# New durations in the price table of a kernel's own list scheduler: a gated scan and two layers on one core

## The chip, the core and the metric

The kernel runs on one core of one Trainium2 chip. The time is the device time of one execution in microseconds; of several runs the median counts.

## The reference

A linear-attention scan over 4 sequences of 768 tokens with 8 heads (32 columns each, a state of 16 rows), then root-mean-square normalisation and a gated layer of 1536 hidden units, then a second layer of 2048 hidden units with squared relu. Shortened to what is computed:

```python
def _attn_ref(x, a, B, C) -> np.ndarray:
    ...
    log_a = np.log(np.clip(a, 1e-06, 1.0))
    state = np.zeros((batch, H, N, D), dtype=np.float32)
    for c in range(nc):
        ...
        cum = np.cumsum(la, axis=-1)
        L = np.exp(cum[:, :, :, None] - cum[:, :, None, :]) * causal
        M = np.einsum('bhin,bhjn->bhij', Cc, Bc) * L
        y[:, :, sl] = (np.einsum('bhij,bhjd->bhid', M, xc)
                       + np.einsum('bhin,bhnd->bhid', Cc, state) * decay_to_i)
        state = decay_full * state + np.sum(Bx, axis=2)
    return y

def _moe_ref(x, w_gate, w_val, w_out, rms_g):
    xn = x / np.sqrt(np.mean(x * x, axis=-1, keepdims=True) + 1e-06) * rms_g
    g = xn @ w_gate
    return (g * (1.0 / (1.0 + np.exp(-g))) * (xn @ w_val)) @ w_out

def _moe2_ref(x, w_in, w_out, s, b):
    r = np.maximum(x @ w_in, 0.0)
    return (s * (r * r) + b) @ w_out

def reference(...):
    attn_out = _attn_ref(x, a, B, C)
    x = attn_out.transpose(0, 2, 1, 3).reshape(3072, 256)
    return _moe2_ref(_moe_ref(x, ...), ...)
```

`x` is (4, 8, 768, 32), `a` (4, 8, 768), `B` and `C` (4, 8, 768, 16); the 3072 tokens then have 256 columns. All inputs are float32; the weights of the layers come as float64.

## The kernel before

**The scan.** The 3072 tokens are cut into 32 chunks of 96 tokens, eight chunks to a sequence, and a chunk's 8 heads are done together. A chunk goes through five steps. `scan` (L381) loads the factors and multiplies them up on VectorE in one instruction over 896 columns (`a<-a,delta`). `gram` (L392) forms the products of B and C on TensorE (`g`) and multiplies them onto the factors on VectorE. `outs` (L413) forms the chunk's output `y` and its next state in eight small products, and ScalarE copies it out (`yt`). `back` (L432) turns it over on TensorE (two transposes, `y<-ident,yt`), copies the state for the next chunk (`xh`), and normalises: ScalarE squares and sums (`xn,ss`), POOL makes the factor in two steps on one column (`ss`, `rs`), and VectorE scales (`xn<-y,rs,gb`; for the first four chunks ScalarE does it). `turn` (L455) turns the normalised chunk back on TensorE (`y<-ident,xn`), and ScalarE and VectorE split it into a high and a low part (`xth`, `xtl`) for the layers. From chunk 7 on `split_bc` (L361) first splits B and C into parts (`hs`, `fb`, `fc`). The bank for `y` exists once: the next chunk's `y` waits until `xth` and `xtl` have been read out of it.

**The layers.** Tokens go in 8 blocks of 384 columns, four chunks each. A product of float32 precision is three products of rounded parts (`three`, L543). `hidden1` and `out1` do layer one, with 12 tiles of 128 hidden units, `hidden2` and `out2` layer two with 16. The first block (`hidden1_plain`, L596) uses plain float32 products in two halves, while the float64 weights are loaded and decoded (`decode`, L487: `e`, `sg`, `raw`, then `w1f` on VectorE and ScalarE). After that the two layers alternate (L713); the chunks of a coming block are scanned while layer two of an earlier one runs, in stretches of about 33 us.

**What sets the order.** The kernel's code is run once against a recorder, `Plan` (L49). Each instruction is written down with a duration from `price` (L140), and with the instructions that it needs. `issue` (L256) then works out starts with a list scheduler: `forward` (L178) starts, engine by engine, the ready instruction with the earliest "latest start", `backward` (L233) works the latest starts out again from the end, three times over, and the best of the three passes is kept. Only the order within each engine reaches the chip; the hardware's semaphores do the waiting. On TensorE products of ones are put into gaps that the schedule shows before the first use of the bank `o0` (L281 to L286), as many as fit the gap at 0.056 us each; they keep the engine going and write into a bank that is not yet used:

```python
while busy + self.FILL + 0.05 < start[i]:
    self.nc.tensor.matmul(out=idle, lhsT=ones, rhs=ones, start=True, stop=True)
    busy += self.FILL * (2 if busy < self.COLD else 1)
```

The price of an instruction thus has two effects: where it and others stand in their engines' queues, and how many products of ones there are. Nearly every instruction is issued from one line, L288 before and L289 after the change.

Of the kernel before, what the change touches and what calls it, by code (L numbers as in the profile page):

```python
# [8 lines left out]
F32 = mybir.dt.float32  # L9
# [10 lines left out]
P = 128  # L20
CH = 96            # tokens of a chunk of the scan
NST = 16           # rows of the scan's state
R = CH + NST       # a chunk's rows: its tokens, then the state
NH = 8
HD = 32
NCHUNK = 32
CPB = 8            # chunks of a batch row
NBLK = 8           # blocks of tokens of the two layers
BCH = NCHUNK // NBLK
N = BCH * CH  # L30
PLAIN = range(7)   # first chunks whose products of B and C are plain float32 ones
LAG = 2
F1 = 12            # tiles of 128 hidden units, first and second layer
F2 = 16
DM = 256
NCLIP = 2          # first chunks whose factors are clipped after they are spread over the rows
SIZE = {F32: 4, F32R: 4, I32: 4, U32: 4, BF16: 2, I16: 2, U16: 2, I64: 8}
EMIN = 916         # a weight's power of two is kept times 2**-20: 16 bits, biased by 127

# [9 lines left out]
class Plan:  # L49
    """Takes instructions down in program order, works out which need which, and issues every  # L50
    engine's in the order in which a list scheduler starts them: of the instructions that are
    ready the one that is to be started first, by the paced products that wait for it."""

    WRITES = ("out", "accum_out")
    FIRST_OUT = ("transpose", "memset", "tensor_copy", "tensor_scalar_mul")
    SEM = 0.13          # us from an instruction's end to a waiting one's start
    DMA_LEAD, DMA_TAIL, DMA_ISSUE, DMA_RATE = 1.1, 0.85, 0.45, 360e3
    BEGIN = 0.6
    COLD = 3.5          # until then the tensor engine runs at half its clock
    FILL = 0.056        # a product in a gap of the tensor engine  # L60
    HOLD = 2.0          # how much longer than the gap left a more urgent instruction may be held up
    STICK = 0.03        # gap in which the next product of a group of small ones is waited for
    PASSES = 3
# [26 lines left out]

    # which bytes of a tile an operand covers: its partitions, and a mask of 4-byte words
    def cover(self, ap):
# [47 lines left out]
    def price(self, eng, fn, args, kw):  # L140
        out = kw.get("out", args[0] if args else None)
        n = out.free_size()
        aps = [a for a in list(args) + list(kw.values()) if hasattr(a, "tensor")]
        psum = any("PSUM" in str(a.space) for a in aps)
        if fn == "dma_start":
            return max(0.06, out.nbytes() / self.DMA_RATE)
        if eng == "tensor":
            if fn == "transpose":
                return max(n / 1.2, 80) / 1e3 + 0.005
            w, four = kw["lhsT"], SIZE[kw["lhsT"].dtype] == 4 and kw["lhsT"].dtype == F32  # L150
            cols = w.free_size()
            if out.start_partition():
                return 0.053
            return max((4 if four else 1) * n / 2.4, (1.64 if four else 0.8) * cols) / 1e3 + 0.003
        if eng == "scalar":
            extra = sum(k in kw and hasattr(kw[k], "tensor") for k in ("scale", "bias", "accum_out"))
            return (n / 1.2 + (51 if psum else 93) + 93 * extra) / 1e3
        if eng == "vector":
            sizes = [SIZE[a.dtype] for a in aps if a.free_size() > 1]
            fast = not psum and fn in ("tensor_scalar", "tensor_copy", "memset")  # L160
            fast = fast or (fn == "tensor_tensor" and not psum and max(sizes) == 2)
            more = 62 if fn == "scalar_tensor_tensor" and hasattr(kw["scalar"], "tensor") else 0
            return (n / (1.92 if fast else 0.96) + 67 + more) / 1e3
        if fn == "tensor_tensor":
            return 0.46
        if fn == "tensor_scalar":
            return 0.16
        return n / 1.15e3 + 0.04
# [7 lines left out]

    # starts and ends, of the ready instructions the one that is to start first going ahead
    def forward(self, succs, late):  # L178
# [52 lines left out]

    # the latest starts with every engine's work in line: a schedule of the same kind from the end
    def backward(self, succs, start, end):  # L233
# [22 lines left out]
    def issue(self, idle):  # L256
        ops = self.ops
        succs = [[] for _ in ops]
        for op in ops:
            for p, lag in op["preds"].items():  # L260
                succs[p].append((op["i"], lag))
        # the latest start that the paced products ask for
        late = [0.0] * len(ops)
# [7 lines left out]
        for _ in range(self.PASSES):  # L271
            start, stop = self.forward(succs, late)
            found.append((max(stop), start, stop))
            late = self.backward(succs, start, max(stop))
        _, start, stop = min(found, key=lambda f: f[0])
        # products of ones in the tensor engine's gaps keep its clock up, until idle is needed
        ones = self.nc.const_aps.tensor(1.0, (P, P), BF16)
        until = min(start[op["i"]] for op in ops if getattr(op["kw"].get("out"), "name", None) == idle.name)
        busy = self.BEGIN
        for op in sorted(ops, key=lambda o: (start[o["i"]], o["i"])):  # L280
# [6 lines left out]
            engine = getattr(self.nc, op["eng"] if op["eng"] != "dma" else "sync")  # L287
# [3 lines left out]
def place(c, h):  # L291
    # where a head's matrix lies: the plain products of even and of odd heads go to two banks
    return h % 2 * 4 + h // 2 if c in PLAIN else h


@with_exitstack
def scan_glu_relu2(ctx: ExitStack, tc: tile.TileContext, bc, xr, aa, cst, w1, w2, gn, sv, bv, out):
# [20 lines left out]
    cst_sb = const.tile([P, 4], F32, name="cst_sb")  # L318
    fc = const.tile([P, 4, 2, R], F32R, name="fc")
    gb = const.tile([CH, DM], F32, name="gb")  # L320
    sb = const.tile([P, 6], F32, name="sb")
# [13 lines left out]

# [1 line left out]
    bc_t, a_t, x_t, f_t, y_t, yt_t, xn_t = {}, {}, {}, {}, {}, {}, {}  # L337
# [21 lines left out]

    # rows of B: hi hi lo lo, of C: hi lo hi lo; a pair of heads has one product  # L360
    def split_bc(c):  # L361
# [112 lines left out]
    def stream():  # L474
        # a chunk's steps lie between those of the chunks before and after it
        s = []
        for c in range(NCHUNK):
            fs = [scan, gram, outs, back, turn]
            at = [2, 4, 7, 9, 11]
            if c not in PLAIN:  # L480
                fs, at = [split_bc] + fs, [0] + at
            s += [(6 * c + t, c, f) for t, f in zip(at, fs)]
        s.sort(key=lambda e: e[0])
        return [(c, f) for _, c, f in s]

# [1 line left out]
    def decode(raw, out, n):  # L487
        # words of a float64: low 32 bits; sign, exponent (11 bits), top 20 bits of the fraction
        low = raw.bitcast(U32).rearrange("p (n w) -> p n w", w=2)[:, :, 0]
# [5 lines left out]
        sg = dec_p.tile([P, 6 * P], BF16, tag="sg", name="sg")[:, :n]  # L495
        # the power of two as the bits of a bfloat16, zero below its range
        nc.vector.tensor_scalar(out=e, in0=top_u, scalar1=0x7FF0, scalar2=None, op0=ALU.bitwise_and)
        nc.scalar.activation(out=e, in_=e, func=AF.Relu, scale=8.0, bias=emin)
        nc.scalar.activation(out=sg, in_=top_i, func=AF.Sign)
        # the mantissa, 2**20 and up  # L500
        nc.vector.tensor_scalar(
            out=high, in0=high, scalar1=0xFFFFF, scalar2=0x100000,
# [3 lines left out]
            out=man, in0=low, scalar=2.0 ** -32, in1=high, op0=ALU.mult, op1=ALU.add  # L506
# [21 lines left out]

    # the second layer's weights stay in the place of their words until they are split
    def decode2(m):  # L530
# [8 lines left out]

# [1 line left out]
    pending = deque()  # L541
# [52 lines left out]

    # the first block, with plain float32 products, in two halves
    def hidden1_plain(j, m, half):  # L596
# [32 lines left out]

    # a further column of ones in the first block sums w2_out's columns  # L630
    def out2(j, m, hi, lo):
# [22 lines left out]
    def drain(n):  # L654
# [10 lines left out]

    # constants
    nc.gpsimd.memset(delta, 0.0)
    nc.gpsimd.affine_select(
        out=delta[0:CH], in_=delta[0:CH], compare_op=ALU.not_equal, fill=1.0, base=0,
# [5 lines left out]
        out=ident, in_=ident, compare_op=ALU.not_equal, fill=1.0, base=0,  # L675
# [17 lines left out]

    # the first block of both layers and the weights, the second block's first layer
    o_t[0, 1] = new_o()
# [6 lines left out]
    for i in range(F1 + behind):  # L702
# [6 lines left out]
        if i >= behind:  # L709
            hidden1_plain(0, i - behind, 1)  # L710
            drain(LAG)
    # the other phases: layer 1 of a block two phases ahead of its layer 2
    phases = [(1, 1), (1, 2), (2, 0), (2, 1)]  # L713
# [6 lines left out]
    start = {(layer, j): i for i, (layer, j, m) in reversed(list(enumerate(plan)))}  # L720
# [88 lines left out]
```

## Time and profile before

| | before |
|---|---|
| time, median of 3 runs | 691.07 us |
| the three runs | 687.67, 691.08, 691.07 us |
| the profiled execution: span from first to last instruction | 687.0 us |
| the profiled execution: its own time from end to end | not given beside its span |
| instructions | 11407 |
| TensorE (PE) busy | 659.5 us, 96% |
| VectorE (DVE) busy | 470.4 us, 68% |
| ScalarE (ACT) busy | 371.1 us, 54% |
| GpSimd (POOL) busy | 65.9 us, 10% |
| products of ones on TensorE | 144 |

Busy shares are means over stages with different limits: the stretches by time say which engine is full where. A wait is put down to the instruction whose end came last. A granted clock of 1.00 is TensorE's upper level, 2.4 GHz, and 0.50 its lower, 1.2 GHz. Products are pipelined, so the time of one in the list is longer than the distance from one to the next.

### The profile page before, as it was taken

What the parts mean: (1) busy time and instruction counts of PE and PEld (TensorE: products, weight loads), DVE (VectorE), ACT (ScalarE), POOL (GpSimd) and SP (SyncE); (2) the same over time, 40 slices, a digit from 0 to 9 for tenths busy, and PEclk for the clock granted to TensorE, in tenths of its full rate; (3) what the DMA queues carried; (4) which work ended last, traced back from release to release, by engine and by line L of the source; (5) the groups of instructions that cost most, each with busy time, mean ns of one, the idle gap of its engine ahead of it and who ended that gap; (6) DMA issues with size and microseconds to landing.
All of it is one profiled execution on the core that took longest, in us unless ns stands there. A gap on an engine that the chain in (4) does not pass through costs nothing.

```text
span 687.0 us, 11407 instructions
## 1 busy us (share of the span) xinstructions
PE 659.5 (96%) x4332; PEld 630.4 (92%) x4332; DVE 470.4 (68%) x832; ACT 371.1 (54%) x780; POOL 65.9 (10%) x112
## 2 busy tenths in 40 slices
PE   8899899999999989999999999999899999999997
PEld 7688699899999879998899989999799998999997
DVE  6789999999997895348933597346963485334443
ACT  3686645667776654356533574346643564335544
POOL 3301210300010130002100030001200011000000
PEclk9899999999999999999999999999999999999999
DMA  8789732300001331004210042002320010000000
GB/s 256 236 294 338 273 113 74 125 1 0 2 1 51 112 113 50 1 1 142 66 42 0 30 141 79 1 1 68 112 68 1 1 59 7 18 1 1 1 23 24
DMA packets 19222, 50.30 MB, mean 73 GB/s; under 512 B 3104, under 2 KB 8576, under 8 KB 19168
## 3 DMA queue, kind: packets, MB, share of 16 engines
q1 hardware_dynamic: 19168, 49.58, 22.4%
q8 instruction: 34, 0.56, 0.3%
q14 instruction: 20, 0.16, 0.1%
HBM read 46.31 MB, written 3.26 MB: 72 GB/s over the span
## 4 chain that ended last, share of the span: by engine, by line
PE 41%; issue 41%; POOL 8%; DVE 6%; ACT 2%; DMA 1%; POOLq 0%; ACTq 0%; DVEq 0%
PE h L288 22%; PE o L288 17%; POOL ss L288 4%; POOL rs L288 4%; DVE a L288 2%; PE y L288 1%; DVE raw L288 1%; DVE e L288 1%; DVE w1f L288 1%; ACT xn L288 1%; DMA a<-in_aa 1%; PE g L288 1%; DMA a<-a_scr 1%; DVE h L288 0%; ACT e L288 0%
## 5 line engine op out<-in xcount | busy, mean ns | idle before, releaser
L288 ACT ACTIVATE s<-h 128x384 f32<-128x384 f32 x212 | 104.1, 491 | 141.3 <-PE h L288 107.9
L288 PE MATMUL h<-x,w2hl 128*128 128x384 f32 x768 | 164.9, 341 | 0.0
L288 DVE TENSOR_TENSOR lo<-s,hi 128x384 fp32r<-128x384 f32 x212 | 117.7, 555 | 39.0 <-ACT hi L288 31.2
L288 PEld LDWEIGHTS h<-x,w2hl 128*128 128x128 f32 x768 | 135.2, 188 | 2.2 <-issue 2.1
L288 PE MATMUL o<-hi,w2hl 128*128 128x384 f32 (+1 forms) x512 | 134.3, 341 | 0.0
L288 PE MATMUL h<-xtl,w1h 128*128 128x384 f32 x336 | 113.3, 337 | 0.9 <-DVE xtl L288 0.9
L288 PE MATMUL h<-xth,w1h 128*128 128x384 f32 x336 | 113.1, 337 | 0.0
L288 PE MATMUL h<-xth,w1l 128*128 128x384 f32 x336 | 113.1, 337 | 0.0
L288 DVE TENSOR_TENSOR s<-h,s 128x384 f32<-128x384 f32 x84 | 46.6, 555 | 70.6 <-PE h L288 66.9
L288 DVE CAST hi<-s 128x384 fp32r<-128x384 f32 x128 | 45.4, 356 | 71.4 <-ACT s L288 69.8
L288 PEld LDWEIGHTS o<-hi,w2hl 128*128 128x128 f32 x512 | 91.9, 188 | 1.6 <-issue 1.4
L288 PE MATMUL o<-lo,w2hl 128*128 128x384 f32 (+1 forms) x256 | 87.2, 343 | 0.0
L288 ACT CAST hi<-s 128x384 fp32r<-128x384 f32 x84 | 43.2, 514 | 78.9 <-DVE s L288 78.6
L288 POOL TENSOR_SCALAR ss<-ss 96x1 f32<-96x1 f32 x32 | 30.2, 943 | 425.8 <-ACT xn L288 424.5
L288 ACT ACTIVATE s<-s 128x384 f32<-128x384 f32 x128 | 67.2, 525 | 3.1
L288 DVE TENSOR_TENSOR_SCAN a<-a,delta 112x896 f32<-112x896 f32 x32 | 64.6, 2019 | 1.3 <-DMA a<-a_scr 1.0
L288 PEld LDWEIGHTS h<-xtl,w1h 128*128 128x128 f32 x336 | 63.1, 188 | 1.9 <-DVE xtl L288 1.5
L288 PEld LDWEIGHTS h<-xth,w1l 128*128 128x128 f32 x336 | 63.1, 188 | 0.2 <-issue 0.2
L288 PEld LDWEIGHTS h<-xth,w1h 128*128 128x128 f32 x336 | 63.1, 188 | 0.0
L288 PE MATMUL o<-lo,w1h 128*128 128x384 f32 x168 | 57.4, 342 | 0.0
L288 PE MATMUL o<-hi,w1h 128*128 128x384 f32 x168 | 56.5, 337 | 0.0
L288 PE MATMUL o<-hi,w1l 128*128 128x384 f32 x168 | 56.4, 336 | 0.0
(68 smaller groups left out, 842.3 us busy)
## 6 DMA issues: line engine op xcount, KB each, us to landing
a<-a_scr SPq DMA_DIRECT2D x30, 392.0 KB, 3.6
bc<-in_bc SPq DMA_DIRECT2D x25, 448.0 KB, 3.8
raw<-in_w SPq DMA_DIRECT2D x12, 768.0 KB, 5.2
raw<-in_w SPq DMA_DIRECT2D x16, 512.0 KB, 6.1
xh<-in_xr SPq DMA_DIRECT2D x32, 96.0 KB, 3.4
out_t<-ob SPq DMA_DIRECT2D x16, 192.0 KB, 1.9
a<-in_aa SPq DMA_DIRECT2D x2, 392.0 KB, 4.9
bc<-in_bc SPq DMA_DIRECT2D x14, 56.0 KB, 5.0
```

Source lines behind the costliest of these rows:

```text
L288: getattr(engine, op["fn"])(*op["args"], **op["kw"])
```

## The change

The prices in `price` are set anew, and nothing else. A product of rounded parts over n columns costs n/2.285 + 6 ns where it was n/2.4 + 3 (384 columns: 174 ns, before 163). ScalarE's base is 60 and 100 ns instead of 51 and 93; an instruction that also sums costs 230 ns more instead of 93, and one that writes fewer than 32 partitions 120 more. VectorE's scan counts twice its columns: 896 columns cost 1.93 us, before 1.00. On POOL the two-input step (`rs`) costs 0.6 us instead of 0.46, and the step with constants (`ss`, one column) falls to the general rule, 0.04 us instead of 0.16. The rest of the diff takes comments away.

```diff
@@ -147,24 +147,25 @@
         if eng == "tensor":
             if fn == "transpose":
                 return max(n / 1.2, 80) / 1e3 + 0.005
-            w, four = kw["lhsT"], SIZE[kw["lhsT"].dtype] == 4 and kw["lhsT"].dtype == F32
+            w, four = kw["lhsT"], kw["lhsT"].dtype == F32
             cols = w.free_size()
             if out.start_partition():
                 return 0.053
-            return max((4 if four else 1) * n / 2.4, (1.64 if four else 0.8) * cols) / 1e3 + 0.003
+            return max(4 * n / 2.4 + 5 if four else n / 2.285 + 6, (1.64 if four else 0.8) * cols) / 1e3
         if eng == "scalar":
-            extra = sum(k in kw and hasattr(kw[k], "tensor") for k in ("scale", "bias", "accum_out"))
-            return (n / 1.2 + (51 if psum else 93) + 93 * extra) / 1e3
+            extra = 93 * sum(k in kw and hasattr(kw[k], "tensor") for k in ("scale", "bias"))
+            extra += 230 if "accum_out" in kw else 120 if out.ap[0][1] < 32 else 0
+            return (n / 1.2 + (60 if psum else 100) + extra) / 1e3
         if eng == "vector":
             sizes = [SIZE[a.dtype] for a in aps if a.free_size() > 1]
             fast = not psum and fn in ("tensor_scalar", "tensor_copy", "memset")
             fast = fast or (fn == "tensor_tensor" and not psum and max(sizes) == 2)
             more = 62 if fn == "scalar_tensor_tensor" and hasattr(kw["scalar"], "tensor") else 0
+            if fn == "tensor_tensor_scan":
+                n *= 2
             return (n / (1.92 if fast else 0.96) + 67 + more) / 1e3
         if fn == "tensor_tensor":
-            return 0.46
-        if fn == "tensor_scalar":
-            return 0.16
+            return 0.6
         return n / 1.15e3 + 0.04
 
     def lasts(self, op, now):
```

The set of instructions is the same but for the products of ones, of which there are now 196 instead of 144. Before, they stand in runs of 33, 43, 7, 15, 3, 15, 20, 7 and 1, all but the last one ahead of the first product of layer one; now in runs of 33, 45, 28, 13, 54 and 13 ahead of those, and 3 and 7 behind the first. POOL's order does not change. On TensorE, VectorE and ScalarE about half the instructions or more change their place, most by a few places; on the queue of SyncE 79 of 156 do.

VectorE in chunk 5 (`a_228` is the factors of chunk 6, `xn_237` the normalised chunk 5, `raw1_279`, `e_281` and `w1f_280` the decoding of the last weight tile of layer one), before:

```order
L288 TENSOR_SCALAR raw1_279<-raw1_279 128x768
L288 TENSOR_TENSOR h32_266<-h_265,h32_266 128x192
L288 SCALAR_TENSOR_TENSOR raw1_279<-raw1_279 128x768
L288 TENSOR_TENSOR e_281<-e_281,sg_282 128x768
L288 SCALAR_TENSOR_TENSOR a_228<-a_228,delta_106 112x896
L288 TENSOR_TENSOR w1f_280<-raw1_279,e_281 128x768
L288 SCALAR_TENSOR_TENSOR xn_237<-y_226,rs_239,gb_104 96x256
```

and now:

```order
L289 TENSOR_SCALAR raw1_279<-raw1_279 128x768
L289 SCALAR_TENSOR_TENSOR a_228<-a_228,delta_106 112x896
L289 SCALAR_TENSOR_TENSOR raw1_279<-raw1_279 128x768
L289 TENSOR_TENSOR e_281<-e_281,sg_282 128x768
L289 TENSOR_TENSOR h32_266<-h_265,h32_266 128x192
L289 TENSOR_TENSOR w1f_280<-raw1_279,e_281 128x768
L289 SCALAR_TENSOR_TENSOR xn_237<-y_226,rs_239,gb_104 96x256
```

The scan of the next chunk stands three instructions earlier.

VectorE at the third chunk under layer two of block 3 (`xn_868` is that chunk, number 18; `a_863` the factors of the next), before:

```order
L288 TENSOR_TENSOR lo_895<-s_893,hi_894 128x384
L288 SCALAR_TENSOR_TENSOR fc_103<-bc_848,cst_sb_102,hs_851 64x4x112 x2
L288 SCALAR_TENSOR_TENSOR a_863<-a_863,delta_106 112x896
L288 CAST hi_901<-s_900 128x384
L288 SCALAR_TENSOR_TENSOR xn_868<-y_857,rs_870,gb_104 96x256
```

and now:

```order
L289 CAST hi_901<-s_900 128x384
L289 TENSOR_TENSOR lo_895<-s_893,hi_894 128x384
L289 SCALAR_TENSOR_TENSOR a_863<-a_863,delta_106 112x896
L289 SCALAR_TENSOR_TENSOR fc_103<-bc_848,cst_sb_102,hs_851 64x4x112 x2
L289 SCALAR_TENSOR_TENSOR xn_868<-y_857,rs_870,gb_104 96x256
```

The scan stands ahead of the two `fc` steps, no longer behind them, and `hi_901` ahead of both. At the last chunk of the stretch, number 19, the scan of the chunk after it now stands directly ahead of `xn_908`, where a `lo` step and an `fc` step lay between.

TensorE at that last chunk (`h_924` and `h_925` are the first products of layer one's next block), before:

```order
L288 MATMUL o0_846<-hi_913,w2hl_643 128x384 x2
L288 MATMUL y_897<-ident_107,xn_908 128x96
L288 MATMUL o0_846<-lo_914,w2hl_643 128x384
L288 MATMUL y_897<-ident_107,xn_908 128x96
L288 MATMUL o1_847<-hi_913,w2hl_643 128x384 x2
L288 MATMUL o1_847<-lo_914,w2hl_643 128x384
L288 MATMUL o0_846<-hi_918,w2hl_649 128x384 x2
L288 MATMUL h_924<-xth_789,w1h0_111 128x384
L288 MATMUL h_924<-xth_789,w1l_306 128x384
```

and now:

```order
L289 MATMUL o0_846<-lo_914,w2hl_643 128x384
L289 MATMUL o1_847<-hi_913,w2hl_643 128x384 x2
L289 MATMUL o1_847<-lo_914,w2hl_643 128x384
L289 MATMUL y_897<-ident_107,xn_908 128x96 x2
L289 MATMUL o0_846<-hi_918,w2hl_649 128x384 x2
L289 MATMUL h_924<-xth_789,w1h0_111 128x384
L289 MATMUL h_924<-xth_789,w1l_306 128x384
L289 MATMUL h_925<-xth_789,w1h0_111 128x384
```

The two transposes of the chunk stand together, three products further back, and two products instead of five lie between them and the first product that reads `xth`. At the third chunk 16 products instead of 13 lie between the transposes of `yt` and those of `xn`, at the last one 16 instead of 17.

## Rows read from the trace of the kernel before

**Rows 1.** The page, busy time, share of the span, instructions.
```profile
PE 659.5 (96%) x4332; PEld 630.4 (92%) x4332; DVE 470.4 (68%) x832; ACT 371.1 (54%) x780; POOL 65.9 (10%) x112
```

**Rows 2.** Chain that ended last: start, us, what; six products.
```profile
182.21 1.05 PE o L288 x6
```

**Rows 3.** Stretches: length, busy us (instructions) of PE, PEld, DVE, ACT, POOL; clock; DMA.
```profile
0.00:40.00 40.00, 33.03 (x347) 28.53 (x348) 29.26 (x38) 22.53 (x46) 13.07 (x21) 0.87 0.79 239
40.00:140.00 100.00, 93.56 (x670) 85.00 (x669) 96.60 (x158) 61.76 (x132) 15.45 (x17) 1.00 0.57 198
140.00:215.00 75.00, 74.96 (x428) 74.67 (x427) 71.78 (x150) 54.05 (x104) 3.40 (x32) 1.00 0.02 7
215.00:580.00 365.00, 354.63 (x2304) 339.22 (x2303) 229.68 (x401) 184.89 (x406) 33.99 (x42) 1.00 0.17 52
```

**Rows 4.** Waits of PE: who waited for whom, us in total, times, longest.
```profile
PE y L288 <- DVE xn L288: 12.4, 16, 1.4
PE y L288 <- ACT xn L288: 3.9, 3, 2.1
```

**Rows 5.** Timeline, chunk 5: the scan, POOL, the transpose that waits.
```profile
73.35 2.01 DVE L288 TENSOR_TENSOR_SCAN a<-a,delta 112x896 f32<-112x896 f32 x1
...
73.73 2.54 POOL L288 TENSOR_SCALAR ss<-ss 96x1 f32<-96x1 f32 x1 [5.75 <-ACT xn L288]
...
77.46 0.38 PE L288 MATMUL y<-ident,xn 96*128 96x96 f32 x2 [1.21 <-DVE xn L288]
```

**Rows 6.** All ss on POOL: ns min/median/max, first and last start.
```profile
L288 POOL TENSOR_SCALAR ss<-ss x32: 187/436/2537, 14.3 to 572.9; 96x1 f32<-96x1 f32 x32
```

**Rows 7.** Timeline, third chunk of one stretch.
```profile
323.20 2.03 DVE L288 TENSOR_TENSOR_SCAN a<-a,delta 112x896 f32<-112x896 f32 x1
...
323.43 2.09 POOL L288 TENSOR_SCALAR ss<-ss 96x1 f32<-96x1 f32 x1 [5.59 <-ACT xn L288]
...
325.60 0.55 POOL L288 TENSOR_TENSOR rs<-ss,fixed 96x1 f32<-96x1 f32 x1
...
326.72 0.38 PE L288 MATMUL y<-ident,xn 96*128 96x96 f32 x2 [1.24 <-DVE xn L288]
```

**Rows 8.** Timeline of PE, start: start, us, what, [idle before <-releaser].
```profile
22.59 0.38 PE L288 MATMUL y<-ident,xn 96*128 96x96 f32 x2 [2.07 <-ACT xn L288]
22.82 0.57 PE L284 MATMUL o<-const-bfloat16-1.0 128*128 128x128 bf16 x7
...
28.63 2.67 PE L288 MATMUL h<-xth,w1f 128*128 128x192 f32 x8
...
37.17 1.46 PE L288 MATMUL h<-xth,w1f 128*128 128x192 f32 x8
```

**Rows 9.** Stretches in the start, columns as in rows 3.
```profile
25.00:31.00 6.00, 6.00 (x44) 4.92 (x43) 5.06 (x7) 3.60 (x8) 1.50 (x1) 0.50 0.49 185
```

**Rows 10.** Timeline, last chunk of the same stretch, into the next block.
```profile
333.94 0.30 PE L288 MATMUL y<-ident,xn 96*128 96x96 f32 x1 [0.62 <-DVE xn L288]
...
334.29 0.25 PE L288 MATMUL y<-ident,xn 96*128 96x96 f32 x1
...
334.57 0.32 ACT L288 CAST xth<-y 128x192 fp32r<-128x192 f32 x1 [0.51 <-PE y L288]
...
335.27 0.33 PE L288 MATMUL h<-xth,w1h 128*128 128x384 f32 x1
```

**Rows 11.** Timeline, second chunk of the same stretch.
```profile
313.01 0.35 DVE L288 TENSOR_TENSOR xtl<-y,xth 128x192 fp32r<-128x192 f32 x1
...
313.28 0.68 DVE L288 SCALAR_TENSOR_TENSOR fb<-bc,cst_sb,hs 128x448 fp32r<-128x448 f32 x1
...
313.86 0.59 PE L288 MATMUL y<-a,xh 112*32 112x112 f32 x16
...
316.07 1.36 DVE L288 SCALAR_TENSOR_TENSOR fc<-bc,cst_sb,hs 64x448 fp32r<-64x448 f32 x2
...
316.87 0.97 POOL L288 TENSOR_TENSOR rs<-ss,fixed 96x1 f32<-96x1 f32 x1
```

## The prediction

> **What bounds the kernel now.** I read the page first. TensorE is busy 96% of the span and no other engine over 68% [rows 1], so the end is set by TensorE's stream of products plus the time in which TensorE stands still. A product of 384 columns follows the last after 1.05/6 = 0.175 us [rows 2]; the change alters no product, so that part stays. What can change is the standing still: 687.0 - 659.5 = 27.5 us in all. Read next where it lies, in the stretches [rows 3]: 40 - 33.0 = 7.0 us in the start, 6.4 us from 40 to 140, nothing from 140 to 215, 10.4 us from 215 to 580; the other 3.7 us are in the tail, where the order is the same but for one product. Then ask what ended the waits [rows 4]: 12.4 us are transposes that wait for a normalised chunk (xn) from VectorE, in 16 places, and 3.9 us the same from ScalarE in the start. The reader should see that the waits are short (1.4 us at most from VectorE) and all at one step of the scan: yt is transposed, squared on ScalarE, two small steps on POOL make ss and rs, VectorE scales xn, and TensorE takes it back.
>
> From 40 to 140 us VectorE is busy 96.6 of 100 us, TensorE 93.6 [rows 3]: there VectorE bounds nearly as hard, and an order can only choose what comes first. From 215 to 580 VectorE is busy 230 of 365 us, and a wait is a matter of order alone.
>
> The long waits for xn have the same picture. In chunk 5 [rows 5] a scan starts on VectorE at 73.35; ss starts on POOL at 73.73 and takes 2.54 us, where the shortest of the 32 takes 0.19 and the middle one 0.44 [rows 6]; the transpose waits 1.21 us. In the third chunk of a stretch [rows 7] it is again a scan (323.20, 2.03 us), with ss under it for 2.09 us, and a wait of 1.24 us. The old table priced that scan at 896/0.96 + 67 = 1000 ns, so the scheduler put it just ahead of a chunk that waits.
>
> **The change, part by part.** The work is the same set of instructions and 52 more products of ones. The sum is made against the span of 687.0 us of the profiled execution; its own end-to-end time is not shown. The median of the three runs, 691.07, lies 4.07 above that span, the fastest run 0.67. I work out the difference on the span and take it from the median.
>
> 1. The start, to 40 us. A product of ones takes 0.57/7 = 0.081 us in a short row [rows 8], the 52 together 4.2. Behind the first product of layer one stand 10 of them, before 1; the rest stand ahead of transposes that wait anyway (2.07 us at 22.59, rows 8). I charge those 9, 0.7 us, and keep 0 and 4.2 as ends. On the other side the granted clock is 0.50, the 1.2 GHz level, from 25 to 31 us at least, and TensorE is never idle in it [rows 9]: 6.0 us of work that takes 3.0 at 2.4 GHz. It shows in two equal rows: eight products take 2.67 us there and 1.46 later [rows 8]. The engine stood still for 2.07 us shortly before the clock fell. The change puts 54 products of ones at that place instead of 20. If the clock then stays up, 3.0 us go; if it falls as before, none. I take half, -1.5, since no row tells which. Together -0.8 us, ends -3.0 and +4.2.
>
> 2. From 40 to 140 us. In chunk 5 the next chunk's scan now has three instructions between it and w1f, where before w1f followed at once; ss then starts after the scan or near its end. Of the 1.21 us [rows 5] I take 0.7 off, because VectorE's queue is full and what goes ahead here is late elsewhere. The other waits there I leave. Ends: 0, and all 6.4 us of the stretch gone [rows 3].
>
> 3. The five stretches between 215 and 580 us in which four chunks each are scanned under layer two. Third chunk: the scan goes ahead of the two fc steps. Before, rs ended 326.15 - 325.23 = 0.92 us after the scan [rows 7] with VectorE all but idle; now the fc steps fill that time, and TensorE has 3 more products between yt and xn, 3 x 0.175 = 0.53 us [rows 2]. 0.92 + 0.53 = 1.45 is more than the wait of 1.24 [rows 7], so the wait goes: five times, -6.2 us. Late next is the last chunk. Its scan now stands directly ahead of xn; I leave its wait of 0.62 [rows 10] as it was, and charge a new one. The next block's first product comes 2 products behind the transposes instead of 5. Before, xth ended at 334.89, 0.60 us after the second transpose started at 334.29, and the product came at 335.27 without a wait [rows 10]. Now the product comes some 0.11 + 2 x 0.175 = 0.46 us after the second transpose starts, against 0.60 and a signal of about 0.1: a wait of 0.24 us, five times, +1.2. In the second chunk xtl goes behind fb, 0.68 us, and the products up to the next y are 3 fewer, 0.53 us. Before, xtl was done 313.86 - 313.36 = 0.50 us ahead of that y [rows 11]. 0.50 - 0.68 - 0.53 would be a wait of 0.7, but xtl's own chain starts earlier by the 3 products that the scheduler took away and put ahead of xn, so I take 0.3: five times, +1.5. Sum of the stretches -6.2 + 1.2 + 1.5 = -3.5 us; ends -8.7 (most waits for xn and no new ones) and +4.
>
> The two POOL steps are priced at 0.64 us together, 0.62 before; the rows show 2.09 + 0.55 under a scan [rows 7], so the new table is as blind to that as the old one. The Trainium skill, in "SBUF — State Buffer", section "Who interferes with whom", says that a VectorE instruction with two SBUF inputs and a GpSimd instruction that reads SBUF shut each other out. The trace agrees as far as the scan goes, which reads a and delta [rows 7]. By that rule every such step on VectorE holds POOL up, the fc steps as well, and to move the scan ahead of them frees nothing; the third chunk would then gain only 5 x 0.53 = 2.7 and part 3 come to nothing. By the new table's prices no wait for xn would be left.
>
> Sum: -0.8 - 0.7 - 3.5 = -5.0 us, 682.0 us of span, **686.1 us** against the median of 691.07. About 0.5% of the time, 3.5 us, is what a measurement of this kernel can tell from no change.
>
> **The rivals.**
>
> *Better than that.* The clock stays up in the start, and the waits for xn fall by 7 us in the stretches without the new ones: -3.0 + 0.7 - 0.7 - 7 = -10.0, 681 us. For it: all prices but POOL's now lie at what the rows show (scan 2.0, product 0.174). Against it: the last chunk's scan ahead of xn.
>
> *Nothing to measure.* POOL stays shut out by what now follows the scan, and the clock falls as before: 0.7 - 0.7 + 0 = 0, 691 us. For it: rs took 0.97 us, not 0.55, while two fc steps ran [rows 11], and VectorE is full to 97% in part 2 [rows 3].
>
> *Slower.* The scan directly ahead of the last chunk's xn sets the pace. If it starts 0.5 us or more after yt's transpose, xn comes only after the whole 2.03 us, then the rest of ss and rs (0.92) and xn itself (about 0.5): 0.5 + 2.03 + 1.4 = 3.9 us, where the 16 products after yt give 2.8 [rows 2, 7]. That is a wait of 1.1 to 1.3 against 0.62 now [rows 10], say 0.6 more; the waits of 0.24 and 0.3 come on top, and the third chunk gains only 0.53: 5 x (0.6 + 0.24 + 0.3 - 0.53) = +3.1, and +0.7 for the ones, 695 us, or 698 with all the ones. If the scan starts before yt's transpose, none of this happens. In the order it stands behind one more step (lo) than before, but yt is transposed five products (0.9 us) later, which speaks against this rival.
>
> **How the numbers follow.** The forecast has 0.44 (its own times 683 to 689), better 0.13 (681), nothing to measure 0.28 (691), slower 0.15 (695). Faster by over 0.5% means below 687.6: three quarters of the forecast (0.33), the better case and a little of the third: 0.49. Slower by over 0.5%, above 694.5: most of the slower case, 0.14. The same: 0.37. The range leaves out a tenth on either side, the far half of the better case and most of the slower one: 680.5 to 693.5.
>
> **What would show it.** In the profile of the changed kernel: the granted clock between 24 and 31 us (1.00 if it stays up), and the first product of layer one at 23 to 24 us as now; waits of TensorE for xn from VectorE of about 6 us in total instead of 12.4; no wait at the third chunk's transpose in each stretch; a new short wait for xth at each change of block; chunk 5's transpose with a wait of half a microsecond. I am wrong if the waits for xn stay at 12 us, if the wait at the last chunk passes 1 us in every stretch, or if TensorE stands still between 140 and 215.

## The result, and the profile after

| | before | after |
|---|---|---|
| time, median | 691.08 us (4 runs, 687.67 to 693.16) | 682.09 us (4 runs, 680.69 to 685.02) |
| ratio, with its 95% interval | | 0.988 [0.9843, 0.9917] |
| profiled execution: span; own time | 687.0; not given | 680.6; 682.6 us |
| PE standing still (span less busy) | 27.5 us | 16.8 us |

The change makes the kernel 1.2% faster: 9.0 us by the medians, 6.4 us by the two profiled spans. The forecast was 686.1 us in a range of 680.5 to 693.5. Ratios here and below are of the means of the fast runs; a slow run (one of e1, 724.01 us, and one of the kernel before in each group beside e9 to e12) counts in a median alone.

The page of the changed kernel, busy time by engine, answers to [rows 1]:

```profile
PE 663.8 (98%) x4384; PEld 635.2 (93%) x4384; DVE 469.4 (69%) x832; ACT 370.9 (54%) x780; POOL 60.6 (9%) x112
```

VectorE and ScalarE do what they did, and POOL's 112 steps take 5.3 us less (65.9 before). PE stands still 10.7 us less; 4.3 us of that are more busy time (52 more products of ones), and 6.4 us are the shorter span. Where it stands still shows in the stretches (columns as in [rows 3]):

```profile
0.00:40.00 40.00, 35.15 (x381) 31.94 (x382) 27.17 (x34) 20.82 (x43) 10.91 (x21) 0.87 0.87 263
40.00:140.00 100.00, 94.98 (x685) 87.36 (x684) 95.83 (x154) 60.41 (x131) 15.89 (x18) 1.00 0.55 188
140.00:215.00 75.00, 75.00 (x429) 74.67 (x429) 74.14 (x157) 56.52 (x108) 4.59 (x32) 1.00 0.03 7
215.00:580.00 365.00, 361.65 (x2341) 344.84 (x2341) 231.38 (x404) 188.48 (x412) 29.21 (x42) 1.00 0.17 54
```

From 215 to 580 us PE's idle time fell from 10.4 to 3.35 us; in the start it fell by 2.1, but there products of ones fill it, and that is no gain. A measure that fillers can't spoil is the time of the first product of layer one in each of the blocks 3 to 7 (the change of block after each of the five stretches). They come at 254.09, 335.27, 415.48, 496.61 and 576.33 us before, and at 253.78, 333.00, 412.43, 491.72 and 569.94 after. So of the 6.4 us, 0.3 come before the first of these marks, 6.1 in the four periods between them (80.56 us on average before, 79.04 after), and none in the tail (110.6 and 110.7 us).

What PE waited for in the changed kernel, answering to [rows 4]:

```profile
PE y L289 <- DVE xn L289: 6.0, 11, 0.8
PE y L289 <- ACT xn L289: 3.2, 2, 1.9
```

The waits for xn from VectorE halved, from 12.4 to 6.0 us, and none is over 0.8. The timeline at the third and the last chunk of the stretch of [rows 7, 10]:

```profile
321.49 2.01 DVE L289 TENSOR_TENSOR_SCAN a<-a,delta 112x896 f32<-112x896 f32 x1
...
322.76 0.72 POOL L289 TENSOR_SCALAR ss<-ss 96x1 f32<-96x1 f32 x1 [5.04 <-ACT xn L289]
...
323.43 1.35 DVE L289 SCALAR_TENSOR_TENSOR fc<-bc,cst_sb,hs 64x448 fp32r<-64x448 f32 x2
...
323.57 0.92 POOL L289 TENSOR_TENSOR rs<-ss,fixed 96x1 f32<-96x1 f32 x1
...
325.35 0.38 PE L289 MATMUL y<-ident,xn 96*128 96x96 f32 x2
...
328.42 0.38 PE L289 MATMUL y<-ident,yt 128*112 128x128 f32 x2
...
329.01 2.01 DVE L289 TENSOR_TENSOR_SCAN a<-a,delta 112x896 f32<-112x896 f32 x1
...
329.76 1.25 POOL L289 TENSOR_SCALAR ss<-ss 96x1 f32<-96x1 f32 x1 [5.27 <-ACT xn L289]
...
332.21 0.38 PE L289 MATMUL y<-ident,xn 96*128 96x96 f32 x2 [0.61 <-DVE xn L289]
...
332.47 0.61 PE L289 MATMUL o<-hi,w2hl 128*128 128x384 f32 x2
...
333.00 0.19 PEld L289 LDWEIGHTS h<-xth,w1h 128*128 128x128 f32 x1 [0.23 <-ACT xth L289]
```

In the third chunk the scan has 0.74 us left when ss starts: ss takes 0.72 us instead of 2.09, rs runs beside the fc steps, and the transpose at 325.35 waits for nothing that the profile counts, where it waited 1.24 us. At the last chunk ss still lies under a scan for 1.25 us, and 0.61 us of waiting stay.

The start. Here PE ran at the granted clock 0.50 (1.2 GHz) in other places than before [rows 8, 9]. Timeline, and two stretches:

```profile
20.52 4.52 PE L285 MATMUL o<-const-bfloat16-1.0 128*128 128x128 bf16 x54
...
24.89 0.33 PE L289 MATMUL y<-ident,xn 96*128 96x96 f32 x2
...
25.82 0.54 PE L289 MATMUL h<-xth,w1f 128*128 128x192 f32 x2
...
29.03 0.34 PE L285 MATMUL o<-const-bfloat16-1.0 128*128 128x128 bf16 x3
...
30.56 0.57 PE L285 MATMUL o<-const-bfloat16-1.0 128*128 128x128 bf16 x7
...
33.03 0.39 PE L289 MATMUL y<-ident,xn 96*128 96x96 f32 x2 [1.90 <-ACT xn L289]
```

```profile
20.00:25.00 5.00, 5.00 (x60) 4.93 (x60) 3.81 (x4) 4.12 (x9) 1.08 (x2) 0.69 0.91 275
...
35.00:40.00 5.00, 5.00 (x31) 4.46 (x30) 2.04 (x4) 2.84 (x8) 0.53 (x2) 0.50 0.77 266
```

The first product of layer one comes at 25.82 us instead of 23.41, and the clock is at its lower level after 33 us, behind a wait of 1.90.

### The profile page after: what moved, and what is told of

It is laid out like the page before. It is cut to its first block, busy times and chain, and to the rows that moved or that the text cites. A ratio compares the mean times of both kernels' runs of the same rounds, so it can differ in the third digit from the quotient of the medians.

```text
span 680.6 us, 11523 instructions
## 1 busy us (share of the span) xinstructions
PE 663.8 (98%) x4384; PEld 635.2 (93%) x4384; DVE 469.4 (69%) x832; ACT 370.9 (54%) x780; POOL 60.6 (9%) x112
## 4 chain that ended last, share of the span: by engine, by line
PE 74%; issue 15%; POOL 7%; ACT 1%; DVE 1%; DMA 1%; POOLq 0%; SPq 0%; ACTq 0%
PE h L289 41%; PE o L289 28%; POOL rs L289 4%; POOL ss L289 3%; PE y L289 3%; PE o L285 2%; PE g L289 1%; DVE xn L289 1%; DMA bc<-in_bc 1%; ACT s L289 0%; ACT xn L289 0%; DMA a<-a_scr 0%; DVE a L289 0%; DVE hi L289 0%; POOL xh L289 0%
## 5 line engine op out<-in xcount | busy, mean ns | idle before, releaser
L289 PE MATMUL o<-hi,w2hl 128*128 128x384 f32 (+1 forms) x512 | 136.2, 342 | 0.0
L289 POOL TENSOR_SCALAR ss<-ss 96x1 f32<-96x1 f32 x32 | 22.4, 699 | 428.0 <-ACT xn L289 308.1
```

The lines of the kernel that those rows point to most:

```text
L289: getattr(engine, op["fn"])(*op["args"], **op["kw"])
```

## The experiments

All ran beside the kernel before, whose median was 689.74 us in the runs of the first four, 690.29 in those of the next four and of the last, and 690.6 in those of e9 to e11. Ratios are to the kernel before in the same group.

| | new prices of | time, us | ratio, 95% interval |
|---|---|---|---|
| e1 | all, order until layer two only | 687.15 | 0.9969 [0.9939, 0.9999] |
| e2 | all, order from layer two on only | 684.27 | 0.9917 [0.988, 0.9954] |
| e3 | scan | 677.44 | 0.9832 [0.9802, 0.9862] |
| e4 | all but the scan | 710.64 | 1.0319 [1.0277, 1.0361] |
| e5 | none; the scan moved by hand | 688.78 | 0.9978 [0.9954, 1.0002] |
| e6 | scan, TensorE | 686.44 | 0.9934 [0.9908, 0.996] |
| e7 | scan, ScalarE | 678.04 | 0.9825 [0.9795, 0.9855] |
| e8 | scan, POOL | 676.36 | 0.9799 [0.9767, 0.983] |
| e9 | all, POOL at the trace's means | 678.67 | 0.9833 [0.9798, 0.9868] |
| e10 | all but TensorE | 675.08 | 0.9784 [0.9753, 0.9816] |
| e11 | all; 34 products of ones fewer | 681.83 | 0.9879 [0.9842, 0.9917] |
| e12 | all but TensorE, POOL at the trace's means | 674.92 | 0.9791 [0.9742, 0.9841] |

**Where the gain lies: e1 and e2.** Both price tables are planned, and the instructions that the new plan starts before 160 us (up to about the first products of layer two) take one plan's order, the others the other's. For e2 the two plans change places.

```diff
+        first, rest = (made[0], made[1])
+        split = [x < self.CUT for x in made[0][0]]
+        start = [first[0][i] if split[i] else rest[0][i] + 1000.0 for i in range(len(ops))]
```

> The order of the change up to the first products of layer two, with its 196 products of ones, and the order of before from there on. Theory (the gain is made in the five stretches under layer two, where waits for xn fell from 8.4 to 2.7 us): no gain here, 690 to 693 us, ratio 0.998 to 1.003, waits of TensorE for xn between 215 and 580 us at 8 us again. Rival (the start and the decoding make the gain, by the ones and the clock): 683 to 686 us, ratio 0.988 to 0.993.

> The reverse: the order of before up to the first products of layer two, with its 144 products of ones, then the order of the change. Theory: all of the gain, 681 to 685 us, ratio 0.986 to 0.991, waits for xn between 215 and 580 us under 3.5 us. Rival: 688 to 691 us, ratio 0.996 to 1.000.

The four periods between the block marks are 322.18 us long in e1, as before (322.24), and 316.13 in e2, as after (316.16): the 6.1 us belong to the later order. What the new start is worth isn't settled. e1's ratio lies between the two ranges that I had expected, and its interval reaches from 0 to 0.6% faster. In the profiled executions of the two kernels chunk 3's transpose in the start comes 3 us later (42.61 after, 39.65 before) and layer two begins 0.57 us later (177.22, 176.65); but in e1's own profile, with the order of the change up to 160 us, layer two begins at 174.12, with a mean granted clock of 0.91 to 40 us where both others have 0.87. Spans of one kernel differ by some us, too: the changed kernel's were 678.7 us at a mean granted clock of 0.995, 680.6 and 679.6 at 0.992, and 683.0 at 0.989.

**Which price: e3 and e4.**

```diff
+            if fn == "tensor_tensor_scan":
+                n *= 2
```

e3 adds these two lines to the kernel before and nothing else; e4 takes them out of the changed one.

> The old table with one price of the new one, the scan at twice its columns (1.93 us instead of 1.00). Theory (the scan's price is what moves it off the chunk that waits): most of the gain, 683 to 687 us, ratio 0.988 to 0.994, ss under 1 us in the third chunk of each stretch. Rival (the products' price, 174 instead of 163 ns, which spaces everything, makes the gain): 689 to 692 us, ratio 0.997 to 1.002.

> The new table with the scan alone at its old price of 1.00 us. Theory: most of the gain is lost, 687 to 691 us, ratio 0.994 to 1.000, the third chunk's ss at 2 us and its wait at 1.2 us again. Rival: 682 to 685 us, ratio 0.987 to 0.992.

The scan's price alone gives more than the whole change by the medians (the intervals of the two ratios overlap between 0.9843 and 0.9862), and without it the other prices cost 3.2%. Both went further than I had expected, e3 by 6 us and e4 by 20. Of the 30.3 us between the spans of e4 and of the changed kernel 9.8 lie ahead of layer two (it begins at 186.98), so the scan's price decides on the start as well. In e4 both inner chunks of a stretch look like the old third chunk; its timeline at one of them:

```profile
330.03 2.02 DVE L287 TENSOR_TENSOR_SCAN a<-a,delta 112x896 f32<-112x896 f32 x1
...
330.23 2.31 POOL L287 TENSOR_SCALAR ss<-ss 96x1 f32<-96x1 f32 x1 [5.49 <-ACT xn L287]
...
333.74 0.38 PE L287 MATMUL y<-ident,xn 96*128 96x96 f32 x2 [1.63 <-DVE xn L287]
```

A scan just ahead of ss, ss under it for 2.31 us, a wait of 1.63, and the same 8 us later (1.65): the scan's old price, all that tells e4 from the change, is what puts it there.

**The move by itself: e5.** The kernel before, with the scan put ahead of the two fc steps in the five third chunks after planning; 15 of 834 places on VectorE differ, and nothing on the other engines.

```diff
+        for c in range(15, 32, 4):
+            k = line.index(scans[c])
+            at = start[line[k - 2]["i"]] - 1e-6
...
+            start[scans[c]["i"]] = at
```

> The kernel before, with one move in VectorE's queue at five places: in the third chunk of each of the five stretches from 215 to 580 us the next chunk's scan goes ahead of the two fc steps instead of behind them (15 of 834 places differ on VectorE; the other engines' orders and the 144 products of ones stay). Theory (what holds POOL's two small steps up is the scan alone): in each of the five places ss and rs are done before the fc steps are, xn starts when they end, 0.92 us earlier than now, and the transposes' wait falls from 1.24 to about 0.3 us: 5 x 0.92 = 4.6 us less, about 685 against 690 us of the kernel before on this chip. Rival (by 'SBUF - State Buffer' of the Trainium skill the fc steps hold POOL up just as long): ss and rs take together over 2 us again, the waits stay at 1.2 us, and the time at 690.

The theory's 685 us did not come: 1.5 us faster by the medians, with an interval that holds no change. By the time alone the rival's 690 us stands; the trace rules its mechanism out. The timeline at the third chunk, and PE's waits:

```profile
323.90 2.02 DVE L295 TENSOR_TENSOR_SCAN a<-a,delta 112x896 f32<-112x896 f32 x1
...
325.54 0.36 POOL L295 TENSOR_SCALAR ss<-ss 96x1 f32<-96x1 f32 x1 [5.58 <-ACT xn L295]
...
325.84 1.35 DVE L295 SCALAR_TENSOR_TENSOR fc<-bc,cst_sb,hs 64x448 fp32r<-64x448 f32 x2
...
325.99 0.91 POOL L295 TENSOR_TENSOR rs<-ss,fixed 96x1 f32<-96x1 f32 x1
...
327.24 0.68 PE L295 MATMUL g<-fc,fb 128*112 128x224 f32 x4 [0.60 <-DVE fc L295]
...
328.28 0.33 PE L295 MATMUL y<-ident,xn 96*128 96x96 f32 x2
```

```profile
PE y L295 <- DVE xn L295: 6.2, 11, 1.2
...
PE g L295 <- DVE fc L295: 3.6, 6, 0.9
```

The wait for xn goes, as the theory has it: ss and rs are through 1.36 us after ss began, inside the fc steps, so the rival is out. But g, the next chunk's products of B and C, needs fc; it stands where it stood, and waits for it 0.6 to 0.9 us in each of the five places. Over half of the 6.2 us that the move takes off the waits for xn comes back there. In the changed kernel g stands further back on TensorE (3.1 us behind the transposes of yt, at 324.83, where it was 2.0). So the move alone is not what pays; that it is the price's moving all queues together is my reading, for no run moves g alone.

**Which of the other prices costs: e6, e7, e8.** Each adds one engine's new lines (as in the change) to e3.

> The scan's new price and TensorE's new prices (384 columns 174 ns), all else at the old prices. The scan's price alone gave 677.4 us, all new prices 682.1, so some 4.7 us are lost by the other three groups of prices. If the products' price is what costs, this comes at about 682, with the 0.6 us wait at the last chunk of each stretch back; if not, at 677 with waits for xn of about 4 us from VectorE.

> The scan's new price and ScalarE's new prices (the step that also sums 230 ns more instead of 93, base 60 and 100 ns), all else at the old prices. If ScalarE's prices are what costs the 4.7 us, this comes at about 682; if not, at 677. The step that sums lies in every chunk's chain just ahead of ss, so I hold this one for the likeliest of the three to bring the 0.6 us wait at the last chunk of each stretch back (5 x 0.6 = 3 us).

> The scan's new price and POOL's new prices (rs 0.6 us instead of 0.46, ss 0.04 instead of 0.16: 0.64 together, 0.62 before), all else at the old prices. Since the two together hardly change, I expect 677 to 678 us; if POOL's prices are what costs the 4.7 us, 682.

I held ScalarE for the likeliest, and it was TensorE: slower than e3 by 9.0 us by the medians and 7.0 by the ratios, while ScalarE's and POOL's prices change nothing that can be measured. Profiled spans differ by less (682.2 and 677.0 us), because e6's profiled run is among its fastest and e3's the slowest of its four. I had 682 us for e6, with the waits of 0.6 us at the last chunk back; they are under 0.3 there, and e6 is 4 us slower than the change, which has ScalarE's and POOL's prices besides. The prices don't add up.

**Why a truer price costs: e9 and e10.** The scheduler lays as many products between a chunk's yt and xn transposes as its prices say are needed. Counted in the orders, for the third and last chunk of the stretch of [rows 7, 10]: 13 and 17 before, 16 and 16 after, 17 and 16 in e3. e9 gives POOL's steps the means of the changed kernel's trace; e10 puts the products back.

```diff
         if fn == "tensor_tensor":
-            return 0.6
+            return 0.9
+        if fn == "tensor_scalar":
+            return 0.7
```

```diff
-            w, four = kw["lhsT"], kw["lhsT"].dtype == F32
+            w, four = kw["lhsT"], SIZE[kw["lhsT"].dtype] == 4 and kw["lhsT"].dtype == F32
...
-            return max(4 * n / 2.4 + 5 if four else n / 2.285 + 6, (1.64 if four else 0.8) * cols) / 1e3
+            return max((4 if four else 1) * n / 2.4, (1.64 if four else 0.8) * cols) / 1e3 + 0.003
```

> The change with POOL's two steps at the means of the changed kernel's trace (ss 0.7 us, rs 0.9 us, 1.6 together; the change has 0.64, and they took 1.60). Theory: the scheduler cuts the distance between a chunk's two transposes to what its prices say, so a chain priced too short, beside a product priced rightly, leaves TensorE waiting at the last chunk of each stretch (0.62 us). With the new price 19 to 21 products lie between the transposes there, where it was 16: the 0.6 us waits of the stretches go, the periods from block to block fall from 79.3 to about 78.3 us, and the time from 682 to 677 or 678 us. Rival: what the products' new price costs lies in the start and in how products stand beside one another, and POOL's price doesn't touch that: 681 to 683 us.

> The change with TensorE's prices put back alone (384 columns 163 ns as before; scan, ScalarE and POOL at the new prices). Theory: the products' new price is what costs against the scan's price alone, since a product priced 7% short makes the scheduler lay more of them between a chunk's transposes (third chunk 21 instead of 16, last chunk 19 instead of 16): no wait for xn over 0.3 us in the stretches, 676 to 678 us. Rival: the loss belongs to the start that this order happened to get, and the time stays at 680 to 683.

The counts are 19 and 21 in e9, 21 and 19 in e10; the times are 3.4 and 7.0 us under the changed kernel's, e9 0.7 us over what I expected and e10 0.9 under. e10's ratio lies clear of the change's; e9's interval overlaps it (0.9798 to 0.9868, 0.9843 to 0.9917). In the profiles e9's span is 4.0 us shorter and e10's 6.4; 1.5 and 1.4 of that lie ahead of layer two, 1.4 and 3.8 in the four periods. The counted waits for xn at the last chunk did not go as I had it: 0.4 us are left in e9 and over 0.5 in e10, in four of the five stretches. Much of e10's gain in the periods is in waits that PE's idle time doesn't show. The row of the weight loader (PEld, the loading of a product's weights) shows more of them; its waits from 215 to 580 us in the changed kernel, and in e10:

```profile
PEld y L289 <- DVE xn L289: 5.5, 9, 0.9
PEld y L289 <- DVE xtl L289: 3.8, 15, 0.3
PEld g L289 <- DVE fc L289: 2.8, 10, 0.5
...
PEld h L289 <- ACT xth L289: 1.2, 5, 0.2
```

```profile
PEld y L289 <- DVE xn L289: 3.4, 4, 0.9
...
PEld y L289 <- DVE lo L289: 1.5, 6, 0.2
...
PEld y L289 <- DVE xtl L289: 0.2, 1, 0.2
PEld h L289 <- ACT xth L289: 0.2, 1, 0.2
```

All the loader's waits of this stretch that another engine's work ended, added up, beside the mean period:

| | PE idle, 215 to 580 us | loader's waits, us | mean period, us |
|---|---|---|---|
| before | 10.4 | 17.4 | 80.56 |
| e5 | 7.3 | 14.1 | 79.92 |
| after | 3.35 | 13.6 | 79.04 |
| e6 | 3.2 | 12.3 | 79.22 |
| e3 | 1.95 | 10.0 | 78.37 |
| e9 | 2.5 | 9.6 | 78.70 |
| e10 | 2.1 | 7.9 | 78.09 |
| e8 | 0.4 | 7.7 | 77.83 |
| e12 | 0.0 | 4.6 | 77.90 |

Both columns put the kernels nearly in the order of their periods, and neither does quite (in both, e6 stands below the change and e12 below e8, though their periods are longer); the loader's waits tell e9 and e10 further apart. The starts of the products settle the size, for they need no modelled end: between the first and the last block mark the 1632 products of 384 columns take 0.175 us each and 15.9 us more before, 10.0 after and 7.6 in e10, and the 64 products of g take 8.5, 7.8 and 6.6 us. From the change to e10 that is 3.6 of the 3.8 us by which the four periods are shorter. One reading is that a product priced 7% short (0.163 us, spaced at 0.175 [rows 2]) acts as a margin wherever a count of products covers a chain, and that a longer price for POOL is another. That fits e9, e10 and e12, and no run varies the margin alone. The counts don't follow the prices so simply: in e8, where POOL's two steps cost 0.02 us more than in e3, 22 products lie at the third chunk instead of 17. In e6 the counts are 17 and 15, e3's but for one product, and new loader waits for yt (2.2 us in five places) stand beside the rest; its longer tail (111.4 us, e3 110.3), where only 0.2 us of waiting is counted, stays open.

**The start's products of ones: e11.** In the changed kernel the second chunk's xn ended 1.3 us before its transposes, which stood behind the 54 ones.

```diff
-                while busy + self.FILL + 0.05 < start[i]:
+                room = 20 if busy > 15 else 99
+                while busy + self.FILL + 0.05 < start[i] and room:
+                    room -= 1
```

> The change with 20 products of ones instead of 54 in the run ahead of the second chunk's transposes in the start (162 in all; no other instruction moves on any engine). In the changed kernel's trace the 54 took 4.52 us at the granted clock 0.50 and ended 1.2 us after the xn was there. Theory: those 1.2 us are lost and come back, 681 us against 682, and the clock is no worse without the 34. Rival (the ones hold the clock up): TensorE then stands still for 1 to 2 us there, the clock falls for longer afterwards, and the time is the same or 1 to 3 us more.

The timeline of PE, and POOL's and ScalarE's step ahead of the last row:

```profile
20.60 2.34 PE L287 MATMUL o<-const-bfloat16-1.0 128*128 128x128 bf16 x20
...
23.71 0.39 PE L291 MATMUL y<-ident,xn 96*128 96x96 f32 x2 [0.77 <-ACT xn L291]
...
24.70 0.56 PE L291 MATMUL h<-xth,w1f 128*128 128x192 f32 x2
...
29.48 3.08 POOL L291 TENSOR_TENSOR rs<-ss,fixed 96x1 f32<-96x1 f32 x1
...
32.58 0.47 ACT L291 ACTIVATE xn<-y,rs 96x256 f32<-96x256 f32 x1 [2.15 <-POOL rs L291]
...
33.11 0.58 PE L291 MATMUL y<-ident,xn 96*128 96x96 f32 x2 [2.60 <-ACT xn L291]
```

The first product of layer one comes 1.1 us earlier, and 8 us on the same transpose waits for the same xn, at 33.11 instead of 33.03. The time is the same. In this start the 34 ones set nothing: TensorE waits for xn, and xn for POOL's rs, which takes 3.08 us here as in the changed kernel. Why it does is not shown.

**Both together: e12.** e10 with POOL's prices of e9.

> Both at once: the change with TensorE's prices put back (163 ns) and POOL's steps at 0.7 and 0.9 us. Theory: each alone took away most of the 0.6 us waits at the last chunk of a stretch; with the products' price put back 0.5 us of it is left per stretch (251.25, 329.59, 408.10, 486.39 us), and 21 products instead of 19 lie between the transposes there now, 17 to 22 at the third chunk: the waits for xn in the stretches fall below 0.3 us, the periods from 78.4 to about 78.0, and the time from 675 to 673 us. Rival: with 29 products between the transposes of the second chunk the y after it comes late, and a wait for fc, xtl or yt takes the place; or the waits were small enough already: 675 to 678 us.

The stretches have no counted idle time left; the window of e12:

```profile
215.00:580.00 365.00, 365.00 (x2381) 352.14 (x2380) 237.07 (x409) 189.55 (x416) 30.89 (x42) 1.00 0.17 54
```

All the same it can't be told from e10 (674.92 and 675.08 us), and the 2 us that I expected on top did not come. Both beat the change by 7 us.

## Why the prediction was right, and where it wasn't

The forecast was 5.0 us less, and it was 9.0; the sign and the range held. That the spans, 6.4 us apart, come so near to 5.0 is in part luck: two terms were off by 2.1 us one way and 3.5 the other. Step by step, on the spans:

**The start and the stretch to 140 us** (-0.8 and -0.7). Measured where layer two begins: +0.6 us in the profiled executions, a pair that doesn't settle it (e1: 174.12). The clock's -1.5 was not seen: the low level moved from 25 to 31 us to other places and stayed (a mean of 0.87 to 40 us in both). The +0.7 for the ones behind the first product wasn't seen either: all 10 of them, at 29.03 and 30.56, stand ahead of the transpose at 33.03, which waits 1.90 us all the same. That the ones ahead of the first product stand before transposes that wait anyway was wrong by 1.3 us at the run of 54, at no cost for the end. Chunk 5's wait went from 1.21 to 0.33 us, as forecast (0.88 where I took 0.7); chunk 4's grew from 0.34 to 0.82 instead.

**The five stretches** (-3.5). Measured from the beginning of layer two to the last block mark: 569.94 - 177.22 against 576.33 - 176.65, -7.0 us. This is the term that was mis-sized, by half. Its main part was right: the third chunk's waits, 1.22 to 1.44 us before, are gone in all five stretches (-6.2 forecast, 6.4 measured), and for rs by the mechanism given, in the time of the fc steps; besides, ss now begins 1.27 us into the scan (322.76 - 321.49) where it was 0.23 [rows 7], so that it lies under its end alone. I left out what those steps, moved back, are late for; e5 shows that g then waits. In the changed kernel, where TensorE's order is new as well, PE counts no wait for fc in the stretches, and the loader 2.8 us (0.6 before).

The two new waits that I charged (+1.2 for xth, +1.5 for xtl in the second chunk) are most of the error, the second above all. The first exists: the loader waits 1.2 us for xth in five places, 0.23 at 333.00, as worked out. After the second transpose two products start, 332.47 + 2 x 0.175 = 332.82, and the next starts at 333.00: 0.18 us a stretch reach the end, 0.9 in all. The second is nearly nothing: ahead of the second chunk's y the loader waits for xtl 0.25 us in all five stretches, where it waited 0.33 to 0.38 in three of them before, 0.2 us more in all against the 1.5. And there was a credit that I did not count. In other places PE's counted waits for xtl (0.78 us at 233.59 among them) went; from 215 to 580 us the changed kernel has none, and the kernel before has these:

```profile
PE h L288 <- DVE xtl L288: 0.9, 2, 0.5
PE y L288 <- DVE xtl L288: 0.8, 1, 0.8
```

The last chunk's wait I left at 0.62 by one stretch. Before, it was 0.34, 0.62, 0.29 and 0.64 us in the first four stretches, and afterwards it is 0.62 in each of them: 0.6 us more in all.

**The base.** The remaining 2.6 us lie between the profiled runs and the medians: the changed kernel's profiled run, 682.6 us, lies 0.5 over its median, and the span of 687.0 before with the same 2.0 us around it would be 689.0, 2.1 under its median. The ratio's interval, 5.7 to 10.8 us, holds both 6.4 and 9.0.

**The rivals.** *Better than that* named 681 us with no new waits and 7 us off the waits in the stretches; this half came true in its size, though the short wait for xth came too, and the clock's half did not. *Nothing to measure* fell, though rs beside the fc steps took 0.92 us, hardly less than its 0.97: ss no longer lay under a whole scan, the two together took 1.64 us where it was 2.64 [rows 7], and the wait went. The Trainium skill's rule behind it ("SBUF — State Buffer", "Who interferes with whom": the two engines shut each other out) still shows in that 0.92 where rs alone takes 0.55 [rows 7]; two short fc steps just cost POOL less than one scan. *Slower* had the right picture at the last chunk (the scan starts at 329.01, 0.59 us after yt's transpose, ss lies under it, xn comes after), and its 3.9 us were nearly right, 332.21 - 328.42 = 3.79. Wrong was the 2.8 us of TensorE's work meanwhile, which took 3.18, the transposes of yt themselves among it: 0.61 of wait instead of 1.1 to 1.3. And the third chunk gained its whole wait.

## What to carry to other kernels

When a scheduler orders a kernel, look for the instruction whose price is furthest from the trace: one such price, half the scan's time, held more than the whole gain here, and the truer price of TensorE's products took some back (e6, e10). A truer price need not give a better order, and an entry that is too low may be the margin that covers what the table doesn't know, so try each entry alone. And before a term counts a step moved back as free, list who reads its result.

## What was not expected of the hardware

PE's idle time is not all its waiting. A product of 384 columns shows some 340 ns in the list and the next may start after 175, so a wait under about 0.17 us hides behind the modelled end; the change and e10 differ by 1.2 us of counted idle time from 215 to 580 us, and by 3.8 us in the four periods. The distances between the products' starts showed the rest, and the weight loader's waits which steps it stood behind.

POOL's one-column steps are long beside other steps than the scan too: in the start of the changed kernel rs took 3.08 us at 29.40 with no scan in that time, beside six VectorE steps of 0.35 to 1.08 us, most of them the decoding of the weights; at 39.66, with VectorE all but idle, it takes 0.55.
